# The normalised attention output in another column order: what VectorE writes and TensorE reads

## The chip, the cores and the metric

The kernel runs on one core of one Trainium2 chip. The metric is the device time of the whole program in microseconds, as a median of runs. The engines of the core are named as in the profile: PE is TensorE (PEld its weight loads), DVE is VectorE, ACT is ScalarE, POOL is GpSimd, and SP issues DMAs.

## The reference

The work has two layers. The first is attention in a window: 8 batches, 8 heads, 576 positions, 64 values a head, where a query sees the keys at most 32 positions away. The second is a mixture of four causal attention experts on its output.

```
def _attn_ref(q, k, v):
    scores = scale * np.matmul(q, k.transpose(0, 1, 3, 2))
    mask = np.abs(pos[:, None] - pos[None, :]) <= 32
    attn = softmax(np.where(mask, scores, -1e9))
    return np.matmul(attn, v)                  # (8, 8, 576, 64)

x = attn_out.transpose(0, 2, 1, 3).reshape(8, 576, 512)
logits = x @ w_gate                            # the best 2 of 4 experts per position
for e in range(4):                             # causal attention of expert e
    ye = softmax(causal(scale * (x @ wq[e]) @ (x @ wk[e]).T)) @ (x @ wv[e]) @ wo[e]
    out += weight_of(e) * ye                   # where e is one of the two
```

(The softmax is written short here.) What matters below is `x`: the normalised attention output, 576 positions by 512 columns for each batch, that must be turned so that the 512 columns lie on the partitions, since all expert products contract over them.

## The kernel before

All engines' work is written out by hand in one list of steps, ORDER (lines 27 to 92). Each step names a function, its batch and tile, sometimes an engine (`:a` ScalarE, `:v` VectorE, `:g` GpSimd), and after `@` the PSUM banks that it uses. The eight PSUM banks are one tile PS, and the list says which step has which bank when. Each engine works through its own steps in the order of the list; the waits between engines follow from what the steps read and write. A load from memory is also held until the TensorE instruction ahead of it in the list is done (`load`, L184).

For each of the 8 batches the steps that touch the change are these:

- `lq`, `lk`, `lv` load queries, keys and values; `tq` and `tk` (`turn`, L293) turn queries and keys on VectorE.
- `sc` multiplies queries with keys on TensorE, `ex` takes the exponential on ScalarE, `mk` applies the window's mask on GpSimd.
- `av` (L349 to L363) multiplies the probabilities with the values, which carry a column of ones as a 65th column. Steps T = 0 to 3 make 128 positions each and fill two banks (8 heads of 65 columns, four in a bank). Step T = 4 has the first and last 32 positions, for both groups of four heads, in one bank.
- `un` (L365) normalises what `av` left in PSUM, on VectorE: a reciprocal of the 65th column into RC, then a multiplication that writes XN (for T = 4 XN2, which the profile also calls XN). There are 4 large ones and one small one for each batch: 32 of 128x512 and 8 of 128x256 in all.
- `xt` (L378) turns XN on TensorE, 128 columns at a time, into PSUM: 8 turns for each of two pairs of T and 2 for T = 4, so 18 for each batch and 144 in all. `turn_pe` (L182) issues them; the profile has all turns at L182.
- `xf` copies the turned tile to XTF, `xb` makes the bf16 copy XTB, on which the expert products (`pp`, `pv`) work; `ga` and the `gt` to `gu` steps compute the gate.

One detail decides the layout. The weights of the second layer are loaded with two neighbouring rows on one partition (for instance L242, `"(g p o) e -> g p o e"` with p = 128 and o = 2): weight rows 256 g + 2 p + o lie on partition p. So turn number dt = 2 g + o has to bring the columns 256 g + o, 256 g + o + 2, and so on to the partitions. Before the change XN holds its columns in their natural order, and each turn reads every second column:

```
XN[w][:, i, 256 * (dt // 2) + dt % 2:256 * (dt // 2) + 256:2]
```

In a turn XN is the weight that TensorE loads, and the identity is the operand that is streamed.

Of the kernel before, what the change touches and what calls it, by code (L numbers as in the profile page):

```python
# [11 lines left out]
MULT = mybir.AluOpType.mult  # L12
# [83 lines left out]
def kernel(  # L96
# [12 lines left out]
    nc = tc.nc  # L109
# [12 lines left out]
    def many(n, shape, dt, name):  # L122
        return [sb.tile(shape, dt, name=f"{name}{i}") for i in range(n)]
# [8 lines left out]
    XN = many(2, [128, 2, DM], F32, "XN")  # L132
    XN2 = sb.tile([128, 256], F32, name="XN2")
# [16 lines left out]
    ident = sb.tile([128, 128], F32, name="ident")  # L150
# [9 lines left out]
    def two(b0):  # L160
        return PS[:, b0:b0 + 2, :]

    def one(b0):
        return PS[:, b0, :]
# [16 lines left out]
    def turn_pe(*a):  # L181
        last_pe[0] = nc.tensor.transpose(*a)  # L182
# [182 lines left out]
    def un(c, b, T, b0):  # L365
        rc = RC[T % 2]
        if T < 4:
            u = two(b0)[:, :, 0:260].rearrange("p g (h c) -> p g h c", c=65)
            nc.vector.reciprocal(rc, u[:, :, :, 64])
            nc.vector.tensor_tensor(out=XN[T // 2][:, T % 2, :].rearrange("p (g h d) -> p g h d", g=2, h=4),  # L370
                                    in0=u[:, :, :, 0:64], in1=rc[:, :, :, None].to_broadcast([128, 2, 4, 64]), op=MULT)
        else:
            u = one(b0)[:, 0:260].rearrange("p (h c) -> p h c", c=65)
            nc.vector.reciprocal(rc[:, 0, :], u[:, :, 64])
            nc.vector.tensor_tensor(out=XN2[:, :].rearrange("p (h d) -> p h d", h=4),
                                    in0=u[:, :, 0:64], in1=rc[:, 0, :, None].to_broadcast([128, 4, 64]), op=MULT)

    def xt(c, b, w, b0):  # L378
        for i in range(2 if w < 2 else 1):
            for dt in range(NDT if w < 2 else 2):  # L380
                turn_pe(PS[:, b0 + i, 128 * dt:128 * dt + 128],
                        XN[w][:, i, 256 * (dt // 2) + dt % 2:256 * (dt // 2) + 256:2] if w < 2 else XN2[:, dt::2], ident)

    ENDS = ((0, 32, 0), (9, 0, 544))

# [214 lines left out]
    with tc.manual_schedule():  # L600
        for step in ORDER.split():
            name, _, banks = step.partition("@")
            name, _, c = name.partition(":")
# [4 lines left out]
            else:  # L608
                op = name.rstrip("0123456789")
# [32 lines left out]
```

## Time and profile before

| what | value |
|---|---|
| median of 3 runs | 244.18 us (244.07 to 247.57) |
| the profiled execution's own time | 243.52 us |
| its span, first to last instruction | 241.5 us |
| mean granted TensorE clock | 0.979 |
| busy: PE / PEld | 218.8 us (91%) / 177.2 us (73%) |
| busy: DVE | 170.9 us (71%) |
| busy: ACT / POOL | 155.3 us (64%) / 157.4 us (65%) |
| XN multiplications on DVE, large | 32, mean 692 ns, 22.1 us busy |
| XN multiplications on DVE, small | 8, mean 424 ns, 3.4 us busy |
| turns of XN on PE | 144, 21.6 us busy |

Busy time is the time in which an engine had at least one instruction under way; matmuls overlap, so the durations of single ones add up to more. Rows of the timeline give start, length, engine, line, operation, output and inputs with their shapes, how many instructions were merged, and in brackets the idle time of the engine just before, with what ended it. The chain that ended last is followed back from the last instruction to whatever released each step.

### The profile page before, as it was taken

What the parts mean: (1) busy time and instruction counts of PE and PEld (TensorE: products, weight loads), DVE (VectorE), ACT (ScalarE), POOL (GpSimd) and SP (SyncE); (2) the same over time, 40 slices, a digit from 0 to 9 for tenths busy, and PEclk for the clock granted to TensorE, in tenths of its full rate; (3) what the DMA queues carried; (4) which work ended last, traced back from release to release, by engine and by line L of the source; (5) the groups of instructions that cost most, each with busy time, mean ns of one, the idle gap of its engine ahead of it and who ended that gap; (6) DMA issues with size and microseconds to landing.
All of it is one profiled execution on the core that took longest, in us unless ns stands there. A gap on an engine that the chain in (4) does not pass through costs nothing.

```text
span 241.5 us, 12394 instructions
## 1 busy us (share of the span) xinstructions
PE 218.8 (91%) x5556; PEld 177.2 (73%) x5556; DVE 170.9 (71%) x351; ACT 155.3 (64%) x241; POOL 157.4 (65%) x193
## 2 busy tenths in 40 slices
PE   0496899899999899999999998999999999999980
PEld 0474787688888688788697976887978877776650
DVE  2976586688789479887975975769745766847660
ACT  2055337868467764769757784988598747757841
POOL 7088928958994879776888953499049993250500
PEclk9998599999999999999999999999999999999997
DMA  6697878866965386568585729636010510332375
GB/s 227 262 214 167 211 201 240 228 178 179 314 140 187 103 251 193 172 182 235 146 259 165 274 62 257 184 102 175 5 26 5 197 71 21 111 111 91 108 282 197
DMA packets 52085, 40.65 MB, mean 168 GB/s; under 512 B 39232, under 2 KB 43328, under 8 KB 52032
## 3 DMA queue, kind: packets, MB, share of 16 engines
q1 hardware_dynamic: 51888, 39.57, 55.3%
q8 instruction: 43, 0.70, 1.2%
q10 hardware_dynamic: 144, 0.29, 0.3%
q14 instruction: 10, 0.08, 0.1%
HBM read 30.42 MB, written 9.44 MB: 165 GB/s over the span
## 4 chain that ended last, share of the span: by engine, by line
PE 80%; DVE 9%; DMA 3%; ACT 3%; issue 3%; ACTq 0%; DVEq 0%
PE PS L179 71%; PE PS L182 9%; DVE Tqn L293 3%; DMA qn<-in_q_dram 2%; DVE Tkn L293 2%; DMA Y<-in_moe_wq_dram 2%; DVE OE L552 1%; ACT V L171 1%; ACT XTF L171 1%; DVE XN L370 1%; ACT ATE L512 0%; ACT XTB L171 0%; DVE PS L428 0%; DVE PS L550 0%; ACT WQ L171 0%
## 5 line engine op out<-in xcount | busy, mean ns | idle before, releaser
L342 POOL TENSOR_TENSOR A<-A,MASKP 128x576 f32<-128x576 f32 x64 | 89.3, 1414 | 23.4 <-ACT A L338 22.8
L179 PE MATMUL PS<-Tqn,Tkn 32*64 32x128 f32 (+3 forms) x2560 | 47.4, 280 | 14.6 <-DVE Tkn L293 11.2
L179 PEld LDWEIGHTS PS<-Tqn,Tkn 32*64 32x64 f32 x2560 | 41.0, 137 | 21.2 <-DVE Tkn L293 12.2
L338 ACT ACTIVATE A<-PS 128x576 f32<-128x576 f32 x64 | 38.5, 649 | 25.2 <-PE PS L179 22.4
L512 ACT ACTIVATE ATE<-PS 128x1024 bf16<-128x1024 f32 x48 | 47.4, 1024 | 10.0 <-PE PS L179 10.0
L517 POOL TENSOR_SCALAR_AFFINE_SELECT ATE<-ATE 128x256 bf16<-128x256 bf16 (+1 forms) x80 | 29.1, 384 | 27.2 <-ACT ATE L512 17.0
L293 DVE STREAM_TRANSPOSE Tkn<-kn 128x576 f32<-128x576 f32 (+1 forms) x34 | 37.4, 1178 | 9.6 <-DMA kn<-in_k_dram 8.1
L293 DVE STREAM_TRANSPOSE Tqn<-qn 128x576 f32<-128x576 f32 (+1 forms) x34 | 37.2, 1179 | 5.8 <-DMA qn<-in_q_dram 4.7
L179 PE MATMUL PS<-V,A 128*64 128x65 f32 (+1 forms) x1280 | 40.1, 226 | 0.8 <-ACT V L171 0.6
L179 PEld LDWEIGHTS PS<-V,A 128*64 128x64 f32 (+1 forms) x1280 | 37.4, 136 | 3.6 <-ACT V L171 0.9
L370 DVE TENSOR_TENSOR XN<-PS,RC 128x512 f32<-128x512 f32 x32 | 22.1, 692 | 1.1
L173 POOL COPY V<-V 64x2048 f32<-64x2048 f32 (+1 forms) x12 | 21.0, 1749 | 3.0 <-DMA V<-in_v_dram 2.4
L173 POOL CAST XTB<-XTF 128x1024 bf16<-128x1024 f32 (+1 forms) x18 | 12.4, 706 | 16.0 <-ACT XTF L171 7.8
L182 PE MATMUL PS<-ident,XN 128*128 128x128 f32 x144 | 21.6, 293 | 0.0
L171 ACT COPY XTF<-PS 128x1024 f32<-128x1024 f32 (+1 forms) x23 | 15.0, 698 | 9.6 <-PE PS L182 9.4
L182 PEld LDWEIGHTS PS<-ident,XN 128*128 128x128 f32 x144 | 18.7, 208 | 2.2 <-DVE XN L370 0.7
L179 PE MATMUL PS<-WO,OTT 128*128 128x512 bf16 (+1 forms) x96 | 19.4, 347 | 0.3 <-DVE OTT L173 0.3
L179 PE MATMUL PS<-WV,XTB 128*128 128x256 bf16 (+1 forms) x192 | 18.6, 256 | 0.1
L171 ACT CAST QKE<-PS 128x576 bf16<-128x576 f32 x21 | 13.4, 643 | 7.5 <-PE PS L179 7.3
L179 PE MATMUL PS<-XTB,WQ 128*128 128x288 bf16 x128 | 17.9, 287 | 0.2 <-ACT A L338 0.2
L171 ACT COPY Y<-PS 128x1024 f32<-128x1024 f32 (+2 forms) x16 | 12.2, 776 | 8.9 <-PE PS L179 8.9
L179 PE MATMUL PS<-XTB,WK 128*128 128x288 bf16 x128 | 17.9, 287 | 0.0
(71 smaller groups left out, 265.0 us busy)
## 6 DMA issues: line engine op xcount, KB each, us to landing
qn<-in_q_dram SPq DMA_DIRECT2D x15, 576.0 KB, 5.1
kn<-in_k_dram SPq DMA_DIRECT2D x15, 576.0 KB, 5.0
V<-in_v_dram SPq DMA_DIRECT2D x32, 256.0 KB, 4.3
out_dram<-Y SPq DMA_DIRECT2D x14, 512.0 KB, 3.4
V<-in_v_dram SPq DMA_DIRECT2D x8, 128.0 KB, 3.1
out_dram<-Y SPq DMA_DIRECT2D x16, 64.0 KB, 2.3
out_dram<-Y SPq DMA_DIRECT2D x4, 256.0 KB, 2.5
kn<-in_k_dram SPq DMA_DIRECT2D x2, 288.0 KB, 4.2
```

The source lines that it names most:

```text
L171: nc.scalar.copy(o, i)
L173: eng(c).tensor_copy(o, i)
L179: last_pe[0] = nc.tensor.matmul(*a, **kw)
L182: last_pe[0] = nc.tensor.transpose(*a)
L293: nc.vector.transpose(T[:, :].rearrange("q (p o) -> q o p", o=18)[:, o0:o1], n_[:, o0:o1, 32 * dh:32 * dh + 32])
L338: nc.scalar.activation(AT[(2 * b + g) % NAT_][half][p], two(b0)[:, :, 0:HS], EXP, scale=scale_att)
L342: eng(c).tensor_tensor(out=ap, in0=ap, in1=MASK[:, None, HS * half:HS * half + HS].to_broadcast([128, 2, HS]), op=MULT)
L370: nc.vector.tensor_tensor(out=XN[T // 2][:, T % 2, :].rearrange("p (g h d) -> p g h d", g=2, h=4), in0=u[:, :, :, 0:64], in1=rc[:, :, :, N ...
L512: nc.scalar.activation(chunk(A, ch), two(b0), EXP, scale=scale_moe)
L517: nc.gpsimd.affine_select(ap, ap, pattern=[[0, n], [1, w]], compare_op=IS_GE, fill=0.0, base=0, channel_multiplier=-1)
L552: nc.vector.tensor_tensor(out=O[:, :, :, :].rearrange("p t e d -> p e t d"), in0=p_[:, :, :, 0:64], in1=rg[:, :, :, None].to_broadcast([12 ...
```

## The change

VectorE writes XN in another order of columns. Column 256 g + 64 h + 2 p + o of the natural order (h counts the four heads of a group, p runs to 32, o is 0 or 1) is stored at 256 g + 128 o + 32 h + p. So the 128 columns of one turn lie side by side, and the turn reads them at a step of one. The multiplication reads PSUM in the same order as before (o fastest), so that the elements it writes one after the other go alternately to the half with o = 0 and the half with o = 1, 128 floats apart. The list of steps, the banks and the number of instructions on each engine are the same, and what comes out of the turns is the same.

```
     def un(c, b, T, b0):
         rc = RC[T % 2]
         if T < 4:
-            u = two(b0)[:, :, 0:260].rearrange("p g (h c) -> p g h c", c=65)
+            u = two(b0)[:, :, 0:260].rearrange("q g (h c) -> q g h c", c=65)
             nc.vector.reciprocal(rc, u[:, :, :, 64])
-            nc.vector.tensor_tensor(out=XN[T // 2][:, T % 2, :].rearrange("p (g h d) -> p g h d", g=2, h=4),
-                                    in0=u[:, :, :, 0:64], in1=rc[:, :, :, None].to_broadcast([128, 2, 4, 64]), op=MULT)
+            nc.vector.tensor_tensor(out=XN[T // 2][:, T % 2, :].rearrange("q (g o h p) -> q g h p o", g=2, o=2, h=4),
+                                    in0=u[:, :, :, 0:64].rearrange("q g h (p o) -> q g h p o", o=2),
+                                    in1=rc[:, :, :, None, None].to_broadcast([128, 2, 4, 32, 2]), op=MULT)
         else:
...
-            nc.vector.tensor_tensor(out=XN2[:, :].rearrange("p (h d) -> p h d", h=4),
-                                    in0=u[:, :, 0:64], in1=rc[:, 0, :, None].to_broadcast([128, 4, 64]), op=MULT)
+            nc.vector.tensor_tensor(out=XN2[:, :].rearrange("q (o h p) -> q h p o", o=2, h=4),
+                                    in0=u[:, :, 0:64].rearrange("q h (p o) -> q h p o", o=2),
+                                    in1=rc[:, 0, :, None, None].to_broadcast([128, 4, 32, 2]), op=MULT)

     def xt(c, b, w, b0):
...
-                        XN[w][:, i, 256 * (dt // 2) + dt % 2:256 * (dt // 2) + 256:2] if w < 2 else XN2[:, dt::2], ident)
+                        XN[w][:, i, 128 * dt:128 * dt + 128] if w < 2 else XN2[:, 128 * dt:128 * dt + 128], ident)
```

More of the change, by code (lines that the diff above doesn't have):

```diff
@@ L367, in un @@
         if T < 4:
-            u = two(b0)[:, :, 0:260].rearrange("p g (h c) -> p g h c", c=65)
+            u = two(b0)[:, :, 0:260].rearrange("q g (h c) -> q g h c", c=65)
             nc.vector.reciprocal(rc, u[:, :, :, 64])
-            nc.vector.tensor_tensor(out=XN[T // 2][:, T % 2, :].rearrange("p (g h d) -> p g h d", g=2, h=4),
-                                    in0=u[:, :, :, 0:64], in1=rc[:, :, :, None].to_broadcast([128, 2, 4, 64]), op=MULT)
+            nc.vector.tensor_tensor(out=XN[T // 2][:, T % 2, :].rearrange("q (g o h p) -> q g h p o", g=2, o=2, h=4),
+                                    in0=u[:, :, :, 0:64].rearrange("q g h (p o) -> q g h p o", o=2),
+                                    in1=rc[:, :, :, None, None].to_broadcast([128, 2, 4, 32, 2]), op=MULT)
         else:
-            u = one(b0)[:, 0:260].rearrange("p (h c) -> p h c", c=65)
+            u = one(b0)[:, 0:260].rearrange("q (h c) -> q h c", c=65)
             nc.vector.reciprocal(rc[:, 0, :], u[:, :, 64])
-            nc.vector.tensor_tensor(out=XN2[:, :].rearrange("p (h d) -> p h d", h=4),
-                                    in0=u[:, :, 0:64], in1=rc[:, 0, :, None].to_broadcast([128, 4, 64]), op=MULT)
+            nc.vector.tensor_tensor(out=XN2[:, :].rearrange("q (o h p) -> q h p o", o=2, h=4),
+                                    in0=u[:, :, 0:64].rearrange("q h (p o) -> q h p o", o=2),
+                                    in1=rc[:, 0, :, None, None].to_broadcast([128, 4, 32, 2]), op=MULT)
     def xt(c, b, w, b0):
```

## The prediction

> **What bounds the kernel now.** I first read the busy times and the chain of the page, then the busy time of the long middle stretch of the span.
>
> ```profile
> span 241.5 us, 12394 instructions
> ...
> PE 218.8 (91%) x5556; PEld 177.2 (73%) x5556; DVE 170.9 (71%) x351; ACT 155.3 (64%) x241; POOL 157.4 (65%) x193
> ...
> PE 80%; DVE 9%; DMA 3%; ACT 3%; issue 3%; ACTq 0%; DVEq 0%
> ```
>
> TensorE (PE) is the bound: 91% of the span and 80% of the chain that ended last. The next row is the busy time from 30 to 210 us (length; then busy us and instructions of PE, PEld, DVE, ACT and POOL; granted clock; DMA share; GB/s).
>
> ```profile
> 30.00:210.00 180.00, 176.16 (x4676) 146.07 (x4673) 136.01 (x276) 127.82 (x200) 129.28 (x148) 1.00 0.56 163
> ```
>
> There TensorE is idle for 180.00 − 176.16 = 3.84 us in all, at a granted clock of 1.00. So a microsecond by which anything makes TensorE late is nearly a microsecond of the end. VectorE (DVE) is idle for 180.00 − 136.01 = 44 us. That is much on average, but what counts is how soon after each VectorE instruction TensorE needs the result or the PSUM bank.
>
> **The change, part by part.** No instruction is added, removed or moved, and no wait or DMA. Two things alter: the order in which 40 VectorE multiplications write their elements (32 on L370, 8 on what is L375 before), and the step at which 144 TensorE turns (L182) read XN: from two floats to one.
>
> *The writes.* Before, each multiplication writes runs of 64 neighbouring floats. After, consecutive elements go alternately to two places 128 floats apart, so no two consecutive writes are neighbours. The reads from PSUM keep their order. These rows are of the view that groups instructions by line and shape (busy us, mean ns of one):
>
> ```profile
> L370 DVE TENSOR_TENSOR XN<-PS,RC 128x512 f32<-128x512 f32 x32 | 22.1, 692 | 1.1
> L375 DVE TENSOR_TENSOR XN<-PS,RC 128x256 f32<-128x256 f32 x8 | 3.4, 424 | 0.3
> L293 DVE STREAM_TRANSPOSE Tqn<-qn 128x576 f32<-128x576 f32 x30 | 34.9, 1242 | 1.2 <-PE PS L179 1.2
> L293 DVE STREAM_TRANSPOSE Tqn<-qn 128x288 f32<-128x288 f32 x4 | 2.3, 707 | 4.7 <-DMA qn<-in_q_dram 4.7
> L428 DVE STREAM_TRANSPOSE PS<-PS 128x160 f32<-128x160 f32 x8 | 3.0, 370 | 3.5 <-PE PS L179 3.5
> L449 DVE TENSOR_TENSOR G<-PS,su 128x20 f32<-128x20 f32 x8 | 1.6, 194 | 0.3
> L442 DVE TENSOR_TENSOR PK<-PS,m 128x20 f32<-128x20 f32 x8 | 1.4, 179 | 0.3
> ```
>
> Today an element costs (692 − 424) / 256 = 1.05 ns, on top of 156 ns that are fixed. Nothing in this trace alternates between two places, but two groups write floats that aren't neighbours. L293 writes at a step of 18 floats, and from its two sizes an element costs (1242 − 707) / 288 = 1.86 ns. That isn't the price of turning as such: L428 turns 160 floats with neighbouring writes in 370 ns, and 160 at 1.86 ns would leave only 72 ns of that as fixed. L449 writes at a step of 5 floats and L442 does the like with neighbours: (194 − 179) / 20 = 0.75 ns more for each element. So scattered writes cost 0.75 to 0.81 ns an element more than neighbouring ones. I take 0.81, from the long rows: L370 becomes 692 + 512 × 0.81 = 1107 ns (+0.41 us), the smaller one 424 + 256 × 0.81 = 631 ns (+0.21 us). Together that is 32 × 0.41 + 8 × 0.21 = 14.8 us of VectorE time. The bounds for the pattern that no row shows: nothing at all, if two alternating places are written as fast as one, and 1.4 ns an element (+0.72 us), a margin of mine of 1.75 times L293's extra, because the two places may collide worse than a step of 18 floats.
>
> [...]
>
> *What of it reaches TensorE.* TensorE's attention products fill two PSUM banks, VectorE normalises them (a reciprocal, then the multiplication), and TensorE soon writes those banks again or turns XN. I followed three of the eight batches through the timeline. Batch 4 first:
>
> ```profile
> 121.77 0.69 DVE L370 TENSOR_TENSOR XN<-PS,RC 128x512 f32<-128x512 f32 x1
> 122.59 0.21 DVE L369 RECIPROCAL RC<-PS 128x8 f32<-128x8 f32 x1
> 122.84 0.69 DVE L370 TENSOR_TENSOR XN<-PS,RC 128x512 f32<-128x512 f32 x1
> 123.45 0.20 DVE L369 RECIPROCAL RC<-PS 128x8 f32<-128x8 f32 x1
> 123.68 0.69 DVE L370 TENSOR_TENSOR XN<-PS,RC 128x512 f32<-128x512 f32 x1
> 124.50 0.21 DVE L369 RECIPROCAL RC<-PS 128x8 f32<-128x8 f32 x1
> 124.74 0.69 DVE L370 TENSOR_TENSOR XN<-PS,RC 128x512 f32<-128x512 f32 x1
> ...
> 124.69 1.23 PE L182 MATMUL PS<-ident,XN 128*128 128x128 f32 x8
> 125.75 0.44 PE L182 MATMUL PS<-ident_bf,OE 128*128 128x128 bf16 x5
> ```
>
> The first multiplication ends at 122.46, 0.13 before the next reciprocal, so that one starts 0.41 − 0.13 = 0.28 late and its multiplication ends 0.69 late. The third follows at once and ends 1.10 late, at 125.47 instead of 124.37. The turns at 124.69 read it: 0.32 of room, so TensorE is 0.78 late. The fourth starts 1.10 − 0.13 = 0.97 late and ends 1.38 late; the turns at 125.75 write its bank, with 0.32 of room: **1.06 us**.
>
> Batch 0:
>
> ```profile
> 30.23 0.21 DVE L369 RECIPROCAL RC<-PS 128x8 f32<-128x8 f32 x1 [0.57 <-PE PS L179]
> 30.47 0.69 DVE L370 TENSOR_TENSOR XN<-PS,RC 128x512 f32<-128x512 f32 x1
> 31.16 0.21 DVE L369 RECIPROCAL RC<-PS 128x8 f32<-128x8 f32 x1
> 31.40 0.69 DVE L370 TENSOR_TENSOR XN<-PS,RC 128x512 f32<-128x512 f32 x1
> 32.02 0.21 DVE L369 RECIPROCAL RC<-PS 128x8 f32<-128x8 f32 x1
> 32.27 0.69 DVE L370 TENSOR_TENSOR XN<-PS,RC 128x512 f32<-128x512 f32 x1
> ...
> 33.12 0.42 DVE L375 TENSOR_TENSOR XN<-PS,RC 128x256 f32<-128x256 f32 x1
> 33.47 2.33 DVE L293 STREAM_TRANSPOSE Tqn<-qn 128x576 f32<-128x576 f32 x2
> ...
> 32.15 0.67 PE L179 MATMUL PS<-V,A 128*32 128x65 f32 x32 [0.17 <-DVE XN L370]
> ...
> 35.85 0.62 PE L179 MATMUL PS<-Tqn,Tkn 32*64 32x64 f32 x25 [0.27 <-DVE Tqn L293]
> ```
>
> The 0.57 us of idle time hides what the first one of the batch loses. From 30.23 on all follow back to back: 0.41, 0.82, 1.23 late, with the small one 1.44. TensorE waits for the second already at 32.15, and at 35.85 for the query turns queued behind all of them, which come 1.44 late: **1.44 us**.
>
> Batch 6:
>
> ```profile
> 170.51 0.69 DVE L370 TENSOR_TENSOR XN<-PS,RC 128x512 f32<-128x512 f32 x1
> 171.34 0.21 DVE L369 RECIPROCAL RC<-PS 128x8 f32<-128x8 f32 x1
> 171.58 0.69 DVE L370 TENSOR_TENSOR XN<-PS,RC 128x512 f32<-128x512 f32 x1
> 172.58 0.21 DVE L369 RECIPROCAL RC<-PS 128x8 f32<-128x8 f32 x1 [0.32 <-ACT Y L171]
> 172.83 0.69 DVE L370 TENSOR_TENSOR XN<-PS,RC 128x512 f32<-128x512 f32 x1
> ...
> 173.87 1.29 PE L179 MATMUL PS<-XTF,WG 128*32 128x160 f32 x32
> ```
>
> Ends late by 0.41, then 0.41 − 0.14 + 0.41 = 0.68, then 0.68 − 0.31 + 0.41 = 0.78; the gate products at 173.87 write the third one's bank with 0.35 of room: **0.43 us**. No turn of XN falls into this stretch, so only the bank counts.
>
> The mean of the three is 0.98 us; 8 × 0.98 = 7.8 us. The rest of the 14.8 us lies in VectorE's own waits. What VectorE does next (key and query turns, the experts' outputs) comes later by the same amount, and so does TensorE, so I count none of it again. Loads wait for TensorE's place in the list, so they shift along.
>
> *The turns.* The rows: the weight loads of the turns in one stretch and of a whole span, and five bf16 turns of the chain of waits (start, length).
>
> ```profile
> 104.74 1.04 PEld L182 LDWEIGHTS PS<-ident,XN 128*128 128x128 f32 x8 [0.24 <-DVE XN L370]
> ...
> L182 PEld LDWEIGHTS PS<-ident,XN 128*128 128x128 f32 x144 | 18.7, 208 | 2.2 <-DVE XN L370 0.7 <-issue 0.6 <-ACT ATE L514 0.3
> ...
> 192.08 0.28 PE PS L182 x5
> ```
>
> XN is the weight, the identity the moving operand. Eight loads start (1.04 − 0.21) / 7 = 0.119 us apart. The gate products above take f32 neighbours as their moving operand: 32 instructions side by side in fours, so eight rounds in 1.29 us; with about 0.30 us for the last to drain (an estimate, from the 0.21 us of a turn's load and the longer stream), (1.29 − 0.30) / 7 = 0.141 us for 160 columns, or 0.113 for 128. So at most 0.119 − 0.113 = 0.006 us of a turn can be the step of two: 144 × 0.006 = 0.9 us. The other end is no gain, and I take half, 0.4 us, because neither row is nearer.
>
> [...]
>
> *The sum.* The profiled execution took 243.52 us with its span of 241.5, and 0.66 us less than the median of 244.18. 243.5 + 7.8 − 0.4 = 250.9 us, and set on the median **251.6 us**, or 3% more. I say 251.5.
>
> **The rivals.**
>
> *The writes are free* (not slower, the other side). If two alternating places are written at the old rate, L370 stays at 692 ns, no batch is late, and what is left is 0 to 0.9 us from the turns: 243.3 to 244.2 us. It decides for the change once the extra is below what the turns give; with 0.32 us of room or less in the batches above, that is an extra under some 0.15 us each. For it: no row alternates. Against it: both rows with scattered writes pay.
>
> *The writes are dearer.* With +0.72 us (and +0.36) the same walk gives 2.3 us in batch 4 (0.72, 0.59 + 0.72, 2.03, 2.62 − 0.32), 2.7 in batch 0 (the first one's idle time is used up, then 0.72 three times and 0.36, with 0.15 brought along), and 1.4 in batch 6 (1.71 − 0.35): 8 × 2.1 = 16.8 us, so 260.6 us. VectorE would then be busy for 171 + 26 us, still under TensorE.
>
> *The lateness is absorbed.* If the batches not walked have room as batch 6 has, and part of TensorE's 3.84 idle microseconds swallows some, 8 × 0.43 − 0.4 = 3 us remain: 247.2 us.
>
> *The turns gain far more than the rows say.* If an f32 turn came down to the bf16 rate (0.28 / 5 = 0.056 us), 144 × 0.063 = 9.1 us would go and 244.18 + 7.8 − 9.1 = 242.9 us be left; with free writes too, 235. Against it: f32 neighbours already stream no faster than 0.113 us for 128 columns.
>
> **How the numbers follow.** Forecast 0.64, around 251.5 (248.5 to 256); dearer writes 0.15; absorbed 0.10; free writes 0.07; fast turns 0.04. The range reaches from 246.5 to 260.0: it holds the forecast, most of the absorbed case and about the dearer case up to its worked time, and leaves out the free writes, the fast turns and a dearer tail. A measurement of this kernel can tell about 2% (4.9 us) from no change, so slower begins at 249.1 us. Slower: 0.64 less a small part under 249.1, with 0.15, gives 0.77. Same: absorbed, free writes, that small part and most of the fast turns: 0.20. Faster by over 2%: 0.03.
>
> **What would show it.** The XN rows of VectorE at about 1107 and 631 ns (at 692 and 424 the writes are free; at 1400 they are the dear kind), and VectorE 171 → about 186 us busy. TensorE's waits for XN and for banks that XN's multiplication releases, 0.7 us on PEld now, should grow to several microseconds, with TensorE's busy time about the same. The turns' loads should start 0.113 to 0.119 us apart. I am wrong if the XN rows grow as said but TensorE in 30 to 210 us has hardly more idle time, or if the turns come out much closer together.

## The result and the profile after

The changed kernel takes 247.74 us (median of 19 runs) where the kernel before takes 244.96 us (19 runs). The ratio is 1.0119 with a 95% interval of 1.0091 to 1.0148: 2.9 us slower (2.2 to 3.6). The forecast was 251.5 us, 3% more. The direction is right and the time lies in the range, but the loss is about two fifths of the 7.3 us that were forecast. It is also within the 2% that had been given a chance of 0.20.

The profiled execution took 248.24 us. First the busy times and the chain that ended last, from its page:

```profile
span 246.2 us, 12394 instructions
...
PE 219.8 (89%) x5556; PEld 175.6 (71%) x5556; DVE 181.8 (74%) x351; ACT 155.7 (63%) x241; POOL 157.3 (64%) x193
...
PE 71%; DVE 20%; issue 4%; DMA 2%; ACT 1%; ACTq 0%; DVEq 0%
PE PS L179 63%; DVE XN L370 8%; PE PS L182 7%; DVE Tqn L293 4%; DVE RC L369 2%; DMA qn<-in_q_dram 2%; DVE Tkn L293 2%; DVE OE L554 1%; ACT ATE L514 1%; DVE XN L376 1%; DVE PS L430 0%; DVE PS L552 0%; DVE QKE L173 0%; ACT Y L171 0%; DVE RG L553 0%
```

VectorE is 10.9 us busier, and its share of the chain went from 9% to 20%: the multiplication into XN alone (L370) now stands for 8% of it. The groups say where the 10.9 us are, and that the turns changed too (busy us, mean ns, idle time before):

```profile
L370 DVE TENSOR_TENSOR XN<-PS,RC 128x512 f32<-128x512 f32 x32 | 34.4, 1074 | 1.1
L376 DVE TENSOR_TENSOR XN<-PS,RC 128x256 f32<-128x256 f32 x8 | 4.9, 616 | 0.3
...
L182 PE MATMUL PS<-ident,XN 128*128 128x128 f32 x144 | 19.8, 279 | 1.5 <-DVE XN L370 1.4
L182 PEld LDWEIGHTS PS<-ident,XN 128*128 128x128 f32 x144 | 15.4, 140 | 4.9 <-DVE XN L370 3.1
```

The large multiplication went from 692 to 1074 ns, the small one from 424 to 616 ns. An element costs (1074 − 616) / 256 = 1.79 ns instead of 1.05. A turn's weight load went from 208 to 140 ns, and the turns are busy for 19.8 us instead of 21.6. The idle time ahead of those loads that ends with XN rose from 0.7 to 3.1 us.

The same stretch from 30 to 210 us as in the prediction (PE, PEld, DVE, ACT, POOL):

```profile
30.00:210.00 180.00, 173.97 (x4620) 142.62 (x4617) 143.72 (x269) 124.48 (x193) 128.89 (x147) 0.99 0.56 162
```

TensorE is idle for 6.0 us there, 2.2 us more than before (in a second trace of the changed kernel, from the run named `after_again` below, 6.9 us).

**What the walk of a batch looks like now.** The timeline of batch 4, VectorE and then TensorE:

```profile
125.74 1.09 DVE L370 TENSOR_TENSOR XN<-PS,RC 128x512 f32<-128x512 f32 x1
126.96 0.21 DVE L369 RECIPROCAL RC<-PS 128x8 f32<-128x8 f32 x1
127.20 1.08 DVE L370 TENSOR_TENSOR XN<-PS,RC 128x512 f32<-128x512 f32 x1
128.14 0.18 DVE L369 RECIPROCAL RC<-PS 128x8 f32<-128x8 f32 x1
128.35 1.05 DVE L370 TENSOR_TENSOR XN<-PS,RC 128x512 f32<-128x512 f32 x1
129.54 0.21 DVE L369 RECIPROCAL RC<-PS 128x8 f32<-128x8 f32 x1
129.78 1.06 DVE L370 TENSOR_TENSOR XN<-PS,RC 128x512 f32<-128x512 f32 x1
...
129.46 1.09 PE L182 MATMUL PS<-ident,XN 128*128 128x128 f32 x8 [0.73 <-DVE XN L370]
130.90 0.44 PE L182 MATMUL PS<-ident_bf,OE 128*128 128x128 bf16 x5 [0.34 <-DVE XN L370]
```

The four multiplications now run into each other, and TensorE stands idle at exactly the two places that were named: 0.73 us ahead of the turns that read the third one, 0.34 us ahead of the turns that write the fourth one's bank. That is 1.07 us; the forecast for this batch was 1.06.

To see all batches I compared the start of the same step in both traces (its first weight load). The column on the right is how much the difference grows between the first and the last step of a batch that VectorE's normalisation touches:

```
batch   from step   before    after   later |  to step    before    after   later | grows by
0       av02         29.89    31.33    1.44 |  sc110       36.73    39.59    2.86 |   1.42
1       av13         46.83    49.34    2.51 |  xt11        53.09    56.72    3.63 |   1.12
2       po00         72.62    76.11    3.49 |  xt21        74.27    78.37    4.10 |   0.61
3       sc401        92.37    95.88    3.51 |  xt30       109.59   113.82    4.23 |   0.72
4       av40        120.26   124.23    3.97 |  xt40       125.98   131.12    5.14 |   1.17
5       pp400       148.18   151.90    3.72 |  xt50       153.22   157.35    4.13 |   0.41
6       av61        169.00   173.03    4.03 |  ga5        173.87   178.24    4.37 |   0.34
7       av71        198.53   202.62    4.09 |  xt71       209.53   214.40    4.86 |   0.77
```

The growth adds up to 6.56 us. Yet the last products (py72) are only 4.73 − 1.44 = 3.29 us later relative to the first row. So some 3.3 us were given back between the batches. About 1.1 us of that is the turns of XN that stand between the rows: the loads of a group of eight in batch 4 start within 0.72 us where they took 0.83. About 1.6 us more is pauses of TensorE that are shorter than before (see below). The rest isn't accounted for. In the second trace the growth is 5.2 us and 2.3 us are given back, and there the turns with 1.1 us and the pauses with 1.2 us are all of it. (The 1.44 us of the first row arose before anything that the change touches; the traces of the other kernels below have between 0 and 2.7 us there. I leave it out.)

Not all of the growth comes from VectorE. In this trace TensorE still ran at half clock when the steps of batch 0 began; before, it didn't. The rows from 31 to 33 us, before and then after (the granted clock is the third number from the end):

```profile
31.00:33.00 2.00, 1.83 (x68) 1.59 (x65) 1.93 (x6) 0.00 (x0) 0.81 (x1) 1.00 0.65 153
```

```profile
31.00:33.00 2.00, 2.00 (x42) 2.00 (x42) 1.58 (x3) 0.00 (x0) 1.68 (x2) 0.50 0.60 188
```

The first step of that batch in the table (av02) took 1.71 us of TensorE instead of 0.93, without waiting. So about 0.8 of batch 0's 1.42 us is clock. In the three other traces with the change's writes in batch 0 (the second one, the writes alone, the change in batches 0, 4 and 6) it grows by 0.84, 0.93 and 1.00 us. Batches 4 and 6 repeat well: 1.17 to 1.20 and 0.34 to 0.36 us in all four traces.

### The profile page after: what moved, and what is told of

Read it like the earlier page. It is cut to its first block, busy times and chain, and to the rows that moved or that the text cites. A ratio compares the mean times of both kernels' runs of the same rounds, so it can differ in the third digit from the quotient of the medians.

```text
span 246.2 us, 12394 instructions
## 1 busy us (share of the span) xinstructions
PE 219.8 (89%) x5556; PEld 175.6 (71%) x5556; DVE 181.8 (74%) x351; ACT 155.7 (63%) x241; POOL 157.3 (64%) x193
## 4 chain that ended last, share of the span: by engine, by line
PE 71%; DVE 20%; issue 4%; DMA 2%; ACT 1%; ACTq 0%; DVEq 0%
PE PS L179 63%; DVE XN L370 8%; PE PS L182 7%; DVE Tqn L293 4%; DVE RC L369 2%; DMA qn<-in_q_dram 2%; DVE Tkn L293 2%; DVE OE L554 1%; ACT ATE L514 1%; DVE XN L376 1%; DVE PS L430 0%; DVE PS L552 0%; DVE QKE L173 0%; ACT Y L171 0%; DVE RG L553 0%
## 5 line engine op out<-in xcount | busy, mean ns | idle before, releaser
L179 PEld LDWEIGHTS PS<-Tqn,Tkn 32*64 32x64 f32 x2560 | 41.3, 137 | 21.6 <-DVE Tkn L293 12.4
L179 PE MATMUL PS<-V,A 128*64 128x65 f32 (+1 forms) x1280 | 41.0, 229 | 1.3 <-DVE RC L369 0.8
L179 PEld LDWEIGHTS PS<-V,A 128*64 128x64 f32 (+1 forms) x1280 | 38.2, 138 | 4.3 <-issue 1.6
L370 DVE TENSOR_TENSOR XN<-PS,RC 128x512 f32<-128x512 f32 x32 | 34.4, 1074 | 1.1
L182 PE MATMUL PS<-ident,XN 128*128 128x128 f32 x144 | 19.8, 279 | 1.5 <-DVE XN L370 1.4
L182 PEld LDWEIGHTS PS<-ident,XN 128*128 128x128 f32 x144 | 15.4, 140 | 4.9 <-DVE XN L370 3.1
L179 PE MATMUL PS<-QKE 64*128 64x64 bf16 (+4 forms) x192 | 17.8, 278 | 1.0 <-DVE RC L375 0.4
```

Of the source, the lines that this page charges most:

```text
L179: last_pe[0] = nc.tensor.matmul(*a, **kw)
```

## The experiments

Theory A, to begin with, says that there are two separate terms, lateness from slower writes and a gain of the turns. The rivals say that one of the two doesn't exist, or that both are large. Each kernel was compared with the kernel before, run beside it.

### The two halves of the change alone, the same lateness by other means, and another way to neighbouring reads

**The writes alone.** The multiplications as after, the turns as before.

```
-        XN[w][:, i, 128 * dt:128 * dt + 128] if w < 2 else XN2[:, 128 * dt:128 * dt + 128], ident)
+        XN[w][:, i, 256 * (dt // 2) + dt % 2:256 * (dt // 2) + 256:2] if w < 2 else XN2[:, dt::2], ident)
```

> VectorE writes XN in pair order as in the changed kernel, the turns keep their step of two floats; the columns that meet a weight row are therefore other ones than in the reference, the amount of work is the same. Theory A (two separate terms: lateness from the slower writes, less a gain of the turns of about 1.2 us): slower than before by 2.8 + 1.2 = 4.0 us, a ratio near 1.016; L370 at 1073 ns, the turns' loads at 209 ns. Rival B (the turns gain nothing that reaches the end, the lateness alone is the measured 2.8 us): ratio 1.012, the same as the changed kernel. Rival C (lateness as forecast, 7.8 us, and the turns gave 5 us back): ratio 1.032.

Measured: ratio 1.0222 (1.0171 to 1.0273), 5.4 us slower. The groups:

```profile
L370 DVE TENSOR_TENSOR XN<-PS,RC 128x512 f32<-128x512 f32 x32 | 34.5, 1078 | 1.1
L376 DVE TENSOR_TENSOR XN<-PS,RC 128x256 f32<-128x256 f32 x8 | 4.9, 616 | 0.3
L182 PEld LDWEIGHTS PS<-ident,XN 128*128 128x128 f32 x144 | 18.8, 208 | 3.7 <-DVE XN L370 2.4 <-issue 0.6 <-DVE XN L376 0.2
```

Rival B falls: the interval lies above 1.012. So does C: 1.032 is outside. Theory A's 1.016 is just below the interval.

**The turns alone.** Read side as after, write side as before.

```
-        XN[w][:, i, 256 * (dt // 2) + dt % 2:256 * (dt // 2) + 256:2] if w < 2 else XN2[:, dt::2], ident)
+        XN[w][:, i, 128 * dt:128 * dt + 128] if w < 2 else XN2[:, 128 * dt:128 * dt + 128], ident)
```

> The turns read 128 neighbouring columns, VectorE writes XN in its natural order as before; the columns that meet a weight row are other ones than in the reference, the amount of work is the same. Theory A: 18 turns a batch come 11 ns closer together and their first load is 70 ns shorter, in all 1.2 us faster, ratio 0.995. Rival B: no change that can be measured, 1.000. Rival C: 5 us faster, 0.980.

Measured: 0.9955 (0.9915 to 0.9995), 1.1 us faster, as A said. B's 1.000 is just outside the interval, C's 0.980 far outside.

```profile
L182 PEld LDWEIGHTS PS<-ident,XN 128*128 128x128 f32 x144 | 15.5, 140 | 2.3 <-DVE XN L370 0.7 <-issue 0.6 <-DVE XN L375 0.3
```

The step of two floats costs a weight load 68 ns: 208 ns on average before, 140 ns here.

**The same lateness without scattered writes.** Each multiplication is followed by a second one that repeats part of it.

```
             nc.vector.tensor_tensor(out=XN[T // 2][:, T % 2, :]..., in0=u[:, :, :, 0:64], ...)
+            nc.vector.tensor_tensor(out=XN[T // 2][:, T % 2, 320:512].rearrange("p (h d) -> p h d", h=3),
+                                    in0=u[:, 1, 1:4, 0:64], in1=rc[:, 1, 1:4, None].to_broadcast([128, 3, 64]), op=MULT)
...
+            nc.vector.tensor_tensor(out=XN2[:, 224:256], in0=u[:, 3, 32:64], in1=rc[:, 0, 3, None].to_broadcast([128, 32]), op=MULT)
```

> Everything as before, but each multiplication into XN is followed by a second one that writes a part of the same values again (192 of 512 columns, or 32 of 256), a little under 0.4 us and 0.2 us of VectorE time, about what the pair order costs, with neighbouring writes and nothing else changed. Theory A (it is lateness of VectorE alone): the same time as with the pair order written and the turns at a step of two, 4.0 us slower than before, ratio 1.016. Rival D (the scattered writes also disturb other engines): this one is slower than before by clearly less than that other kernel. Rival C: 7.8 us slower, 1.032.

Measured: 1.0178 (1.0124 to 1.0231), 4.3 us slower; the added instructions are these:

```profile
L372 DVE TENSOR_TENSOR XN<-PS,RC 128x192 f32<-128x192 f32 x32 | 11.4, 357 | 1.1
...
L379 DVE TENSOR_TENSOR XN<-PS,RC 128x32 f32<-128x32 f32 x8 | 1.5, 191 | 0.3
```

The intervals of this kernel and of the writes alone overlap widely. So VectorE's added time by itself accounts for the loss, as far as the intervals can tell (4.3 of 5.4 us), and nothing here shows that the scattered writes disturb another engine (rival D). C's 1.032 is out again.

**Neighbouring reads by another row order of the weights.** XN stays in natural order; the weights and the gate are loaded so that row 128 t + p lies on partition p.

```
-            load(WG[:, 2 * g:2 * g + 2, 0:4], moe_w_gate.rearrange("(g p o) e -> g p o e", p=128, o=2)[g])
+        load(WG[:, :, 0:4], moe_w_gate.rearrange("(t p) e -> p t e", p=128))
...
-             (moe_wq, moe_wk)[n][2 * j:2 * j + 2].rearrange("e (g p o) d -> p (e g) (o d)", p=128, o=2))
+             (moe_wq, moe_wk)[n][2 * j:2 * j + 2].rearrange("e (t p) d -> p (e t) d", p=128))
```

(The load of wv likewise, and the turns as after.)

> XN stays in its natural order and the turns read neighbours; instead of XN the weights of the second layer and of the gate are loaded with row 128 t + p on partition p, in runs of 256 bytes instead of 512. It computes what the reference does. Theory A: the gain of the turns without the price of the writes, 1.2 us faster than before, ratio 0.995, if the twice as many packets of the weight loads stay hidden. Rival: the weight loads land later (0.5 to 2 us) and hold up the copies of the weights early in the kernel, ratio 1.000 to 1.008.

Measured: 0.9956 (0.9917 to 0.9994). Its trace has 55140 DMA packets, the trace of before 52085. The kernel has the gain of the turns and no price on VectorE; the rival's 1.000 to 1.008 is just outside. It was run again beside the kernels of the last round:

> The kernel with the weights loaded in another row order once more, beside the others, to narrow its interval: ratio 0.995; a ratio of 1.000 would say that the first measurement was chance.

Measured: 0.9974 (0.9923 to 1.0026). Both agree with 0.995 to 0.997, but the second interval reaches past 1, so the rival isn't out by it. It beats the changed kernel clearly, the kernel before by about 0.3%, at the limit of what these runs can tell.

What the two halves say together: 5.4 − 1.1 = 4.3 us for the whole, or with the delay alone 4.3 − 1.1 = 3.2. The whole was 2.9 us at first, and 3.5 us when it was run again:

> The changed kernel itself, beside the others. From its first measurement a ratio of 1.012. If the parts that were tried alone simply add (0.0087 and 0.0140), 1.023; if they had been measured on slower ground, 1.012 again.

Measured: 1.0143 (1.0093 to 1.0194). So the terms are a lateness of 4.3 to 5.4 us and a gain of 1.1 us. A lateness of 7.8 us is outside both intervals. What had become of the rest was open.

### Which batches, and is the rest a fixed amount or a share?

**The change in some batches only.** `un` and `xt` take the new form for the batches in a list, the old one for the others.

```
+    PAIR = (0, 4, 6)
+    def un(c, b, T, b0):
+        (un_pair if b in PAIR else un_nat)(c, b, T, b0)
+    def xt(c, b, w, b0):
+        (xt_pair if b in PAIR else xt_nat)(c, b, w, b0)
```

> The change in batches 0, 4 and 6 alone (writes and turns), the other five as before; it computes what the reference does. Theory E (TensorE's own pauses of 0.2 to 0.8 us inside the query-key products, released by nothing in the trace, shrink when TensorE arrives late): these three batches make TensorE 2.4 to 3.0 us late in the traces so far, and the pauses behind batches 2, 4 and 5 give about 1.5 us back: 0.9 to 1.5 us slower than before, ratio 1.004 to 1.006. Rival F (nothing is given back): 2.4 to 3.0 us slower, ratio 1.010 to 1.012.

> The change in batches 1, 2, 3, 5 and 7 alone; it computes what the reference does. Theory E: 3.0 to 3.8 us of lateness, of which the same pauses swallow about 1.5 us: 1.5 to 2.3 us slower, ratio 1.006 to 1.009; with the other kernel's part it adds up to less than or about the whole change. Rival G (the mean of the walked three holds for these too, 5 times 0.98 us less the gain of the turns): 4.2 us slower, ratio 1.017.

Measured: 1.0087 (1.0047 to 1.0128) for batches 0, 4 and 6, which is 2.1 us, 0.7 us a batch; 1.0140 (1.0093 to 1.0187) for the other five, 3.4 us, 0.7 us a batch. The interval of the first holds F's values (1.010 to 1.012) wholly and E's (1.004 to 1.006) for the most part. That of the second has G's 1.017 inside and E's upper end, 1.009, just outside. So the five batches lose about as much each as the walked three, in time; the difference that the trace of after shows (0.73 us of growth against 0.98, part of it the clock in batch 0) isn't confirmed by these runs. The two parts add up to 5.5 us where the whole is 2.9 to 3.5. That is the opposite of E's "less than or about". The gap is less sure than it looks: taken from the medians, the parts lose 2.5 and 2.8 us, and the whole 2.8 and 4.1.

**Twice the delay.**

```
+            for _ in range(2):
                 nc.vector.tensor_tensor(out=XN[T // 2][:, T % 2, 320:512]...
```

> As the kernel with the delay alone, but the second, partial multiplication is issued twice, so each normalisation costs about 0.76 us more than before instead of 0.38. Theory E (a fixed amount is swallowed once, about 3.4 us of a walked 7.5 us): walked for all eight batches with 0.75 us the lateness is 16.8 us, less 3.4 us is 13.4 us slower, ratio 1.055. Rival H (a fixed share of the lateness reaches the end): twice the 4.3 us of the single delay, 8.6 us slower, ratio 1.035.

Measured: 1.0735 (1.0679 to 1.0791), 17.9 us slower. Both theories are wrong, H by far. The second helping of the same work on VectorE, 32 × 0.357 + 8 × 0.191 = 12.9 us by the rows above, and a little more with the gaps between instructions, costs 17.9 − 4.3 = 13.6 us, with about 2 us of uncertainty; the two profiled executions differ by 10.4 us. So most or all of it reaches the end. Of the first helping about a third does. That would fit a fixed amount of room, about 9 us of VectorE time over the 40 normalisations or a little over 0.2 us for each on average; two sizes of the delay can't show more than that. My walk with 0.75 us gave 16.8 us, close to 17.9; with 0.38 us it gave 7.5 us where 4.3 were measured. It fails for the small delay and nearly holds for the large one. The waits of TensorE on XN, by the view of who waited for whom, are now many:

```profile
PE PS L179 <- DVE XN L373: 4.7, 11, 0.6
PE PS L179 <- DVE XN L370: 2.4, 4, 1.3
PE PS L182 <- DVE XN L381: 1.6, 1, 1.6
```

**Pair order without scattered writes.** The multiplication writes one half of the pairs behind the other and so reads PSUM at a step of two; three dimensions then need two instructions, one for each group of heads.

```
+            for g in range(2):
+                nc.vector.tensor_tensor(out=XN[T // 2][:, T % 2, 256 * g:256 * g + 256].rearrange("q (o h p) -> q o h p", o=2, h=4),
+                                        in0=u[:, g, :, 0:64].rearrange("q h (p o) -> q o h p", o=2),
+                                        in1=rc[:, g, None, :, None].to_broadcast([128, 2, 4, 32]), op=MULT)
```

> XN in pair order and turns that read neighbours, as in the changed kernel, but the multiplication writes one half of the pairs after the other, so that it writes runs of 128 neighbours and reads PSUM at a step of two floats; for that each large multiplication is two of 256 columns, one for each group of four heads. It computes what the reference does. Theory (the price is in the scattered writes, a PSUM read at a step of two is free): 2 x 424 ns instead of 692, about 0.2 us later for each; the pauses swallow most of it and the turns give 1.1 us back: 0.5 us faster to 0.5 us slower, ratio 0.998 to 1.002, and the small multiplication stays at 424 ns. Rival I (any step costs as the writes did): 2 x 613 ns, ratio above 1.03, the small one at 613 ns.

Measured: 0.9999 (0.9962 to 1.0035).

```profile
L371 DVE TENSOR_TENSOR XN<-PS,RC 128x256 f32<-128x256 f32 x64 | 24.1, 418 | 1.1
L377 DVE TENSOR_TENSOR XN<-PS,RC 128x256 f32<-128x256 f32 x8 | 3.4, 424 | 0.3
```

The small multiplication is back at 424 ns, so a read of PSUM at a step of two floats costs nothing here, and the price was in the writes. The whole loss of the change is gone, with the same layout of XN, although the two instructions take 2 × 418 ns where one took 692.

### TensorE's own pauses

In the trace of before TensorE pauses four times between 30 and 240 us, for 2.2 us in all, where nothing that the profile shows releases it. The view of who waited for whom has them as "issue". Before, and then after:

```profile
PE PS L179 <- issue: 2.2, 4, 0.8
```

```profile
PE PS L179 <- issue: 0.5, 2, 0.4
```

Two of them lie inside query-key products, which write banks that a normalisation has just read. Before:

```profile
80.04 1.26 PE L179 MATMUL PS<-Tqn,Tkn 32*64 32x160 f32 x60 [0.76 <-issue]
...
147.88 0.37 PE L179 MATMUL PS<-Tqn,Tkn 32*64 32x96 f32 x2 [0.75 <-issue]
```

After, the first is 0.16 us and the second is gone (in the second trace of the same kernel the first is gone and the second is 0.39 us):

```profile
83.68 1.07 PE L179 MATMUL PS<-Tqn,Tkn 32*64 32x160 f32 x53 [0.16 <-issue]
```

Theory E: what comes late just ahead of such a pause shortens it. The same added work at two pairs of places was to show it:

```
+            for _ in range(2 if (b, T) in ((2, 0), (5, 0)) else 0):     # elsewhere: ((3, 3), (7, 2))
+                nc.vector.tensor_tensor(out=XN[T // 2][:, T % 2, 320:512]...
```

> Everything as before, but two of the 40 normalisations write a part of their columns twice more (0.76 us of VectorE time each): those of batch 2 and batch 5, T = 0, whose banks the query-key products with a pause at 79.3 and at 147.1 us write next, with 0.14 and 0.03 us of room. Theory E (the pause swallows what comes late just ahead of it): TensorE starts those products 0.6 to 0.7 us later and pauses that much less, 0 to 0.2 us at the end, ratio 1.000 to 1.001, and the waits of TensorE that nothing releases fall from 2.2 us to about 0.8. Rival F (the pauses stay): 1.35 us slower, ratio 1.0055, and those waits stay at 2.2 us.

> Everything as before, but two other normalisations write a part of their columns twice more: batch 3, T = 3, and batch 7, T = 2, behind which turns wait with 0.17 and 0.10 us of room and no pause follows. Both theories: TensorE 0.59 + 0.66 = 1.25 us later, ratio 1.005, and the waits that nothing releases stay near 2.2 us.

Measured: 1.0014 (0.9976 to 1.0053) ahead of the pauses, 1.0059 (1.0029 to 1.0088) elsewhere. Both points are near where E has them; the intervals overlap, and 1.0055, which F gives for the first, is just outside. The medians of the two kernels lie only 0.6 us apart, so the times alone decide little. In the trace of the first, TensorE waits for the late multiplication and doesn't pause later in the same products:

```profile
80.39 2.89 PE L179 MATMUL PS<-Tqn,Tkn 32*64 32x64 f32 x147 [0.36 <-DVE XN L373]
...
147.28 1.32 PE L179 MATMUL PS<-Tqn,Tkn 32*64 32x64 f32 x74 [0.46 <-DVE XN L373]
```

and the waits that nothing releases are down to 0.3 us. But in the trace of the second kernel they are down too, to 0.5 us, against what both theories said:

```profile
PE PS L179 <- issue: 0.5, 1, 0.5
```

So these pauses also come and go by themselves: the traces of the kernels without added lateness (before, the turns alone, the weights' order twice) have 2.2, 2.9, 2.2 and 1.4 us, those with lateness in all batches (the change twice, the writes alone, the delay, twice the delay) 0.5, 1.0, 0.5, 0.2 and none, pair order without scattered writes 1.4, the two with the change in some batches 2.2 and 1.7. That lateness shortens them is what most traces say; these sums don't settle it.

What goes with them can be read from the traces together. The 14 traces hold 32 such pauses of more than 0.15 us between 30 and 240 us. The profile lists a DMA queue (q8) of the kind "instruction", with 43 packets of 16 KB in each trace, 3.2 to 9.8 us apart. Every one of the 32 pauses ends 2.2 to 2.8 us after such a packet starts (in the trace of before, packets at 77.67 and at 145.24 us, pauses that end at 80.04 and at 147.88). And every one stands at the same place in a count of TensorE's instructions, 188 to 194 behind a multiple of 256: in the trace of before after 3777, 5826, 6594 and 7618 of them. TensorE's 167 waits of that length for another engine or a DMA have no such pattern; they end 0.0 to 7.3 us after the last packet, and at many places in the count. A reading that would fit both, a guess of mine, is that TensorE pauses where its next instructions have not arrived; then what delays it between the start of the packet and that place would come out of the pause, as in the trace with the late multiplications above. No run here shows it: none changed how instructions are loaded, and why a packet starts early in one execution and late in another stays open.

## Why the prediction was right or wrong

**The price of a scattered write** was right: 1107 and 631 ns forecast, 1074 and 616 measured. What was read from transposes with a step of 18 floats (0.81 ns more an element), and from 20 elements of the gate (0.75), held for a pattern that no row showed (0.74); that it carries over so closely is in part luck. In all an element costs 1.79 ns at hops of 512 bytes, where neighbours cost 1.05. The free writes and the dear ones are both out.

**Where TensorE would wait** was right in batches 4 and 6: they grow by 1.17 and 0.34 us, and the walk had 1.06 and 0.43. In batch 0 the walk was too long. Its 1.44 us meets the 1.42 us of the trace, but there about 0.8 us is the half clock, and the three other traces have 0.84 to 1.00. That the three batches come to 2.93 us in the trace and in the walk is luck.

**"8 × 0.98 us; I count none of it again" was the step that failed**, with the sentence on which it stands: that a microsecond by which TensorE is late is nearly a microsecond of the end. The two kernels with the lateness alone, the delay and the writes, lose 4.3 and 5.4 us, not 7.8. The step went wrong in three places. The 0.98 us had batch 0 in it, at about half a microsecond too much. The five batches that weren't walked grow by 3.63 us in the trace of after, and by 2.8 in the second trace, instead of 4.9. And not all of what had grown stayed: TensorE's pauses are 1.7 us shorter in the trace of after (2.2 to 0.5) and 1.2 in the second; that a late TensorE finds its instructions loaded is my guess at it, which no run shows. I had set TensorE's 3.84 idle microseconds aside as small; against a loss of 7 us they aren't. The rival in which the lateness is absorbed, at 247.2 us with a chance of 0.10, came nearest to the 247.7 us.

**The gain of the turns was mis-sized**: 0.4 us taken, 0.9 at most, 1.1 us measured (0.1 to 2.1), and 1.8 us less busy time of TensorE in the trace of after (21.6 to 19.8). The bound of 0.113 us for a turn came from gate products whose last instruction I let drain for an estimated 0.30 us; in the trace of before one of them lasts 0.299 us in the median. The turns of batch 4 in fact start 0.109 us apart, where it was 0.120 before, and each load is 68 ns shorter as well; the first turn of that group lasts 0.33 us instead of 0.39. Eight turns that took 1.23 us of TensorE in the prediction's stretch now take 1.09 us (both are rows of batch 4).

The sum, with the measured terms: 4.3 to 5.4 us of lateness less 1.1 us of turns gives 3.2 to 4.3 us, and the change itself measured 2.9 and 3.5 us. What isn't explained is why the change in three batches and in the other five, tried apart, cost 2.1 and 3.4 us, 5.5 together. About 1 us of the gap is the pauses: against before they are 0.0 and 0.5 us shorter in the traces of the two parts, and 1.2 to 1.7 us in those of the whole.

Of the signs that were named, VectorE's busy time (181.8 for a forecast 186 us) and the idle time before the turns' loads that XN ends (0.7 to 3.1 us) came as said. The sign against me came too: in 30 to 210 us TensorE has only 2.2 us more idle time, and 3.1 in the second trace.

## What to carry to other kernels

Here a read made contiguous on one engine (a weight load of a turn: 208 to 140 ns) by letting another engine's writes jump (a large multiplication: 692 to 1074 ns) cost 2.9 us; look for an order in which both sides keep runs. The loads of the weights (once for the whole kernel) could take the reordering (ratios 0.9956 and 0.9974), or PSUM reads at a step of two, which were free (418 and 424 ns for 256 elements, 424 before; ratio 0.9999). When a slower instruction off the bound is walked through a schedule, the walk can find the right waits and still come to too large a sum when the delay is of the size of the room: here 0.38 us for each normalisation cost a third of itself at the end, and the next 0.38 us cost most or all of itself. And before a row of one trace is taken to confirm a forecast, look at its granted clock and at a second trace of the same kernel.

## What the runs showed of the hardware that was not expected

- A weight load of 128 f32 columns of XN took 208 ns at a step of two floats (before, the writes alone) and 140 ns at a step of one (after, the turns alone).
- The VectorE multiplication out of PSUM read at a step of two floats as fast as at one (418 and 424 ns for 256 elements, 424 at one), while writes that alternate between two places 512 bytes apart cost 1.79 ns an element against 1.05.
- TensorE paused for 0.16 to 1.2 us with nothing in the profile's waits that releases it, in sum none to 2.9 us of an execution, and differently in two executions of the same kernel (0.5 and 1.0 us). All 32 such pauses stand at steps of 256 in a count of TensorE's instructions and end 2.2 to 2.8 us after a 16 KB packet starts in the queue of the kind "instruction".
- The granted TensorE clock near the start was 0.50 for a stretch that ended at another time in each of three executions: at about 30 us in the trace of before, 33 us in that of after, 31 us in the second trace of the same kernel.
